# Fourth chunk's mask ahead of waiting sums, warm matmuls, and output matmuls of the second token tile over the end of the first

## The chip, the cores and the metric

One core of a Trainium2 chip. The time is device microseconds (us) of one execution; the profile's span is about 1.8 us shorter (230.7 against 232.52 for the profiled execution of the kernel before). PE is TensorE, PEld its weight loads, DVE VectorE, ACT ScalarE, POOL GpSimd.

## The reference, cut to what matters

```python
for t in range(S):                                   # decayed linear attention, 8 heads, S = 768, D = 64
    state = gamma * state + outer(k[t], v[t])
    y[t] = scale * q[t] @ state
x = y as (3072 tokens, 512)
h = x @ w_in                                         # 512 -> 2048
g = h + sin(alpha * h) ** 2 / (alpha + 1e-9)
out = g @ w_out                                      # 2048 -> 512
```

## The kernel before

The attention is done in 24 chunks of 128 tokens. `stage_T` (or two `half_T`) transposes q and k of a chunk, `stage_A` makes the scores `pa` and masks them on DVE into `aT`, `stage_M` multiplies with v into `py` and copies the result to `xT`. Chunks are gathered in groups (4, 2, 4, ... chunks); for each group the feed-forward layer runs over 16 blocks f of 128 hidden units:

```python
def ff_in(g, f, square, cols=None):
    ph = psum.tile([128, hi - lo], F32, name="ph", tag="mm", bufs=4)     # ring of four PSUM banks
    s = work.tile([128, hi - lo], F32, name="s", tag="s", bufs=4)
    for i in range(KS):
        nc.tensor.matmul(ph, w_in[:, i, ...f...], xT[g][:, i, lo:hi], ...)
    nc.scalar.activation(out=s, in_=ph, func=ACTF.Sin, scale=alpha_sb[:, f:f + 1])
    if square == "A":  nc.scalar.activation(out=s, in_=s, func=ACTF.Square)
    else:              nc.vector.tensor_mul(s, s, s)
    return lambda: nc.vector.scalar_tensor_tensor(gT[g][:, f, lo:hi], s, rec_alpha, ph, ...)   # "the sum"

def ff_out(g, ts, f):                       # one output matmul po; po also takes a bank of the ring "mm"
    nc.tensor.matmul(po[g, ts], gT[g][:, f, ts * C:(ts + 1) * C], w_out[:, f, :], ...)
```

"The sum of f" below is that last DVE instruction, which also frees the bank of ph. The first group has no earlier group to hide behind. Its first three chunks run through f = 0 to 5 while the fourth chunk (`e3`) arrives; then the fourth chunk's 128 columns run through f = 0 to 5 (`second tile`), then all 512 columns through f = 6 to 15:

```python
decay_table(3)
for f in range(4):
    ff_in(0, f, "AAD"[f % 3], (0, n3))()
half_T(e3, 0, nc.vector); half_T(e3, 1, nc.vector)
idle_work(2)                                # 2 matmuls on zeros, the "warm matmuls"
for f in range(4, early):
    ff_in(0, f, "AAD"[f % 3], (0, n3))()    # the trailing () issues the sum at once
    if f == 4:
        stage_A(e3)
stage_M(e3); decay_table(4); idle_work(3)
for f in range(early):
    ff_in(0, f, "AD"[f % 2], (n3, 4 * C))()
    if f in (2, 3, 4, 5):
        ff_out(0, 0, f - 2)
# ... scaling of v, two memsets, decay_table(5)
phase(0, [... ff_out(0, 0, f) for f in range(4, FF - 2)], {}, "AAD", range(early, FF))
outs = [... ff_out(0, 0, f) for f in range(FF - 2, FF)] + out_pieces(0, (1, 2, 3))
fill(9); stage_T(P[4]); scale_v(P[4], nc.vector); fill(5); stage_A(P[4])   # fill(n): n items of outs
```

Of the kernel before, what the change touches and what calls it, by code (L numbers as in the profile page):

```python
# [15 lines left out]
def kernel(  # L16
# [15 lines left out]
    nc = tc.nc  # L32
    B, H, S, D = q.shape
    C = 128
# [6 lines left out]
    FF = d_ff // 128  # L41
# [64 lines left out]
    def scale_v(j, eng):  # L106
        eng.tensor_mul(raw["v", j], raw["v", j], kg[:, j % NCH, :, None].to_broadcast([128, H, D]))  # L107
# [51 lines left out]
    def decay_table(c):  # L159
        nc.vector.tensor_mul(qg[:, c], qg[:, 0], step[:, c, :, None].to_broadcast([128, NP, C]))  # L160
# [11 lines left out]
    def half_T(j, i, eng):  # L172

        if i == 0:
            st["qkT", j] = work.tile([128, 2 * NP, 128], BF16, name="qkT", tag="qkT", bufs=3)
        pt = psum.tile([128, NP, 128], BF16, name="pt", tag="mm", bufs=4)
        for p in range(NP):
            nc.tensor.transpose(pt[:, p, :], raw["qk"[i], j][:, 2 * p:2 * p + 2, :].rearrange("p h d -> p (h d)"), ident)
        o = st["qkT", j][:, i * NP:(i + 1) * NP, :]
        if eng is nc.scalar:  # L180
            nc.scalar.copy(o, pt)
        else:
            nc.vector.tensor_copy(o, pt)

    def stage_T(j):
        pt = psum.tile([128, 2 * NP, 128], BF16, name="pt", tag="ty")
        st["qkT", j] = work.tile([128, 2 * NP, 128], BF16, name="qkT", tag="qkT", bufs=3)
        for i in range(2):
            for p in range(NP):
                nc.tensor.transpose(pt[:, i * NP + p, :],  # L190
                                    raw["qk"[i], j][:, 2 * p:2 * p + 2, :].rearrange("p h d -> p (h d)"), ident)
        nc.vector.tensor_copy(st["qkT", j], pt)  # L192

    def stage_A(j):
        qkT = st["qkT", j]
        pa = psum.tile([128, 2, NP, 128], F32, name="pa", tag="pa")
        for p in range(NP):
            for e in range(2):
                r = slice(64 * e, 64 * e + 64)
                nc.tensor.matmul(pa[:, e, p, :], qkT[r, NP + p, :], qkT[r, p, :],  # L200
                                 start=(p == 0), stop=True, skip_group_check=True)
        aT = work.tile([128, 2, NP, 128], BF16, name="aT", tag="aT", bufs=2)
        m = dec.rearrange("p e n t -> p (e n) t") if j % NCH == 0 else mask_bc
        nc.vector.tensor_mul(aT.rearrange("p e n t -> p (e n) t"), pa.rearrange("p e n t -> p (e n) t"), m)  # L204
        st["aT", j] = aT

    def stage_S(j):
        c = j % NCH
        if c == 0:
            st["ps"] = psum.tile([128, NP, D], F32, name="ps", tag="ps")  # L210
        ps = st["ps"]
        for p in range(NP):
            for e in range(2):
                nc.tensor.matmul(ps[64 * e:64 * e + 64, p, :], raw["k", j][:, 2 * p + e, :], raw["v", j][:, 2 * p + e, :],  # L214
                                 start=(c == 0 and p == 0), stop=True, skip_group_check=True)
        return ps

    def keep_S(j, ps):
        for e in range(2):
            r = slice(64 * e, 64 * e + 64)  # L220
            nc.scalar.copy(s_bd[(j % NCH + 1) % 2][r, :, r], ps[r, :, :])  # L221

    def stage_M(j):
        c = j % NCH
        g, i = place[j]
        if g not in xT:
            xT[g] = work.tile([128, KS, sizes[g] * C], BF16, name="xT", tag="xT", bufs=3)
        qkT, aT, vs = st["qkT", j], st["aT", j], raw["v", j]
        py = psum.tile([128, NP, 128], F32, name="py", tag="ty")
        if c > 0:  # L230
            for p in range(NP):
                for e in range(2):
                    r = slice(64 * e, 64 * e + 64)
                    nc.tensor.matmul(py[r, p, :], s_bd[c % 2][:, p, r], qkT[:, p, :],  # L234
                                     start=(p == 0), stop=True, skip_group_check=True)
        for p in range(NP):
            for e in range(2):
                nc.tensor.matmul(py[64 * e:64 * e + 64, p, :], vs[:, 2 * p + e, :], aT[:, e, p, :],  # L238
                                 start=(c == 0 and p == 0), stop=True, skip_group_check=True)
        x = xT[g][:, :, i * C:(i + 1) * C]  # L240
        if c == 0:
            nc.scalar.copy(x, py)
            return
        ps = stage_S(j) if c < NCH - 1 else None
        nc.vector.tensor_mul(x, py, qg[:, c])  # L245
        if ps is not None:
            keep_S(j, ps)
# [4 lines left out]
    def ff_in(g, f, square, cols=None):  # L252
        n = sizes[g] * C
        lo, hi = cols or (0, n)
        if g not in gT:
            gT[g] = work.tile([128, FF, n], BF16, name="gT", tag="gT", bufs=2)
        ph = psum.tile([128, hi - lo], F32, name="ph", tag="mm", bufs=4)
        s = work.tile([128, hi - lo], F32, name="s", tag="s", bufs=4)
        for i in range(KS):
            nc.tensor.matmul(ph, w_in[:, i, f * 128:(f + 1) * 128], xT[g][:, i, lo:hi],  # L260
                             start=(i == 0), stop=(i == KS - 1))
        nc.scalar.activation(out=s, in_=ph, func=ACTF.Sin, scale=alpha_sb[:, f:f + 1])  # L262
        if square == "A":
            nc.scalar.activation(out=s, in_=s, func=ACTF.Square)  # L264
        else:
            nc.vector.tensor_mul(s, s, s)
        return lambda: nc.vector.scalar_tensor_tensor(  # L267
            gT[g][:, f, lo:hi], s, rec_alpha[:, f:f + 1], ph, op0=ALU.mult, op1=ALU.add)
# [5 lines left out]
    def ff_out(g, ts, f):  # L274
        if f == 0:
            po[g, ts] = psum.tile([128, d_model], F32, name="po", tag="mm", bufs=4)
        nc.tensor.matmul(po[g, ts], gT[g][:, f, ts * C:(ts + 1) * C], w_out[:, f, :],  # L277
                         start=(f == 0), stop=(f == FF - 1))
        if f == FF - 1:
            o_sb = work.tile([128, d_model], F32, name="o_sb", tag="o_sb", bufs=3)  # L280
            o_dram = out_view[:, groups[g][ts], :]
            if (g, ts) == end:
                h = d_model // 2
                nc.vector.tensor_copy(o_sb[:, :h], po[g, ts][:, :h])
                nc.scalar.copy(o_sb[:, h:], po[g, ts][:, h:])
            else:
                nc.scalar.copy(o_sb, po[g, ts])  # L287
            nc.sync.dma_start(out=o_dram, in_=o_sb)

    def out_pieces(g, tss):  # L290
        return [lambda ts=ts, f=f: ff_out(g, ts, f) for ts in tss for f in range(FF)]
# [5 lines left out]
    def idle_work(n):  # L297
        for _ in range(n):
            nc.tensor.matmul(spare["ps"], warm[:, :128], warm, start=True, stop=True)  # L299
# [5 lines left out]
    e0, e1, e2, e3 = order[:B]  # L305
# [41 lines left out]
    def phase(g, outs, att, squares, slots=range(FF)):  # L347

        no, n0, done = len(outs), len(slots), 0
        for n, f in enumerate(slots):  # L350
            add = ff_in(g, f, squares[f % len(squares)])
            for fn in att.get(f, ()):
                fn()
            add()
            while done < no * (n + 1) // n0:
                outs[done]()
                done += 1
# [18 lines left out]


    n3, early = 3 * C, 6
    decay_table(3)
    for f in range(4):  # L380
        ff_in(0, f, "AAD"[f % 3], (0, n3))()
    half_T(e3, 0, nc.vector)
    half_T(e3, 1, nc.vector)
    idle_work(2)
    for f in range(4, early):
        ff_in(0, f, "AAD"[f % 3], (0, n3))()
        if f == 4:
            stage_A(e3)
    stage_M(e3)
    decay_table(4)  # L390
    idle_work(3)
    for f in range(early):
        ff_in(0, f, "AD"[f % 2], (n3, 4 * C))()
        if f in (2, 3, 4, 5):
            ff_out(0, 0, f - 2)
    scale_v(e0, nc.vector)
    for t in s_bd:
        nc.vector.memset(t, 0.0)
    decay_table(5)
    P = order  # L400
    phase(0, [lambda f=f: ff_out(0, 0, f) for f in range(4, FF - 2)], {}, "AAD", range(early, FF))
    outs = [lambda f=f: ff_out(0, 0, f) for f in range(FF - 2, FF)] + out_pieces(0, (1, 2, 3))

    def fill(n):
        for _ in range(n):
            outs.pop(0)()
# [7 lines left out]
        if n in (13, 15, 17):  # L414
            scale_v(order[(n - 11) // 2], nc.gpsimd)

    fill(9)
    stage_T(P[4])
    scale_v(P[4], nc.vector)
    fill(5)  # L420
# [7 lines left out]
    stage_M(P[4])  # L428
    fill(6)
    stage_M(P[5])  # L430
    fill(4)
    phase(1, outs,
          {0: [T(P[6])], 2: [A(P[6])], 3: [T(P[7])], 5: [A(P[7]), M(P[6])], 7: [T(P[8])],
           9: [A(P[8]), M(P[7])], 11: [T(P[9])], 13: [A(P[9]), M(P[8]), SK(P[9] - 1)], 15: [M(P[9])]}, "A")
# [46 lines left out]
```

## Time and profile before

| | before |
|---|---|
| median of four runs | 231.68 us (231.13 to 232.51) |
| span of the profile | 230.7 us |
| PE busy | 94% |
| PE waits before 46 us that could move | 1.92, 0.99 and 0.63 us |
| half clock | one stretch of 3.41 us, 25.75 to 29.16 us |

A line of the timeline reads: start in us, length in us, engine, line of the program, instruction, output<-inputs, shapes, number of instructions merged; in brackets the idle time of the engine before it and what ended it. The prediction shows the lines for the waits and the clock. What it shows only in numbers is the loop f = 6 to 15; here it is for f = 9 in the timeline of the kernel before:

```profile
33.00 1.03 PE L260 MATMUL ph<-xT,w_in 128*128 128x512 bf16 x4
34.07 0.69 ACT L262 ACTIVATE s<-ph,alpha_sb 128x512 f32<-128x512 f32 x1 [0.52 <-PE ph L260]
34.79 0.63 ACT L264 ACTIVATE s<-s 128x512 f32<-128x512 f32 x1
35.45 0.75 DVE L267 SCALAR_TENSOR_TENSOR gT<-s,rec_alpha,ph 128x512 bf16<-128x512 f32 x1 [0.31 <-ACT s L264]
36.29 0.38 PE L277 MATMUL po<-w_out,gT 128*128 128x512 bf16 x1
36.51 1.03 PE L260 MATMUL ph<-xT,w_in 128*128 128x512 bf16 x4
```

ph of f = 9 starts at 33.00; its sine, square and sum follow one after another; po of f = 9 can start only when the sum has ended (36.20), and ph of f = 12 stands behind it. From ph to ph of three f later: 3.51 us, 1.17 per f, though PE's own work is 1.08.

### The profile page before, as it was taken

Reading aid. Unit: us, or ns where it says so; the run is one execution under the profiler, and the core shown is the slowest. Engines: PE = TensorE matmul, PEld = TensorE weight load, DVE = VectorE, ACT = ScalarE, POOL = GpSimd, SP = SyncE. Lnnn points to the kernel's source line nnn. Section 1 sums busy time; section 2 is a strip of 40 time slices with the busy share of each in tenths; the row PEclk is TensorE's granted clock in tenths of the full one; section 3 lists DMA queues with packets and bytes.
Section 4 is the critical chain, followed back from the end, with each engine's and each line's share of the span. In section 5 each row is a group of like instructions: output and inputs, shape, how many; then the busy total and the mean of one; then the engine's idle time right before and its main releaser. Section 6 shows DMA issues by size and latency. Waiting matters only on the chain.

```text
span 230.7 us, 4496 instructions
## 1 busy us (share of the span) xinstructions
PE 217.7 (94%) x1786; PEld 115.0 (50%) x1786; DVE 143.6 (62%) x234; ACT 167.2 (72%) x323; POOL 90.3 (39%) x105
## 2 busy tenths in 40 slices
PE   7995799799999999999999999999999999999992
PEld 3542543356775555545454544554544454556540
DVE  4776887595987777866575755674764554533400
ACT  7786479436898899877787777787677878777720
POOL 8955437899999999992000000000000000000000
PEclk9999799999999999999999999999999999999999
DMA  9999999999999999996110110011011011111111
GB/s 130 150 190 198 205 199 156 154 186 135 139 94 126 115 91 154 107 124 57 45 48 8 40 47 24 24 47 45 3 45 48 0 45 45 48 45 45 50 66 70
DMA packets 82613, 20.49 MB, mean 89 GB/s; under 512 B 75408, under 2 KB 79520, under 8 KB 82592
## 3 DMA queue, kind: packets, MB, share of 16 engines
q0 software_dynamic: 77024, 13.37, 74.2%
q1 hardware_dynamic: 5568, 6.83, 8.7%
q8 instruction: 14, 0.23, 0.4%
q14 instruction: 7, 0.06, 0.1%
HBM read 27.27 MB, written 6.29 MB: 145 GB/s over the span
## 4 chain that ended last, share of the span: by engine, by line
PE 79%; DVE 7%; DMA 4%; POOL 4%; ACT 4%; issue 1%; POOLq 0%
PE po L277 36%; PE ph L260 31%; DMA kr<-in_k_dram 4%; PE pt L190 4%; PE pa L200 2%; PE py L234 2%; DVE aT L204 2%; DVE gT L267 2%; ACT s L262 2%; PE py L238 2%; ACT s L264 1%; POOL vr L78 1%; POOL qr L78 1%; DVE xT L245 1%; PE ps L214 1%
## 5 line engine op out<-in xcount | busy, mean ns | idle before, releaser
L267 DVE SCALAR_TENSOR_TENSOR gT<-s,rec_alpha,ph 128x512 bf16<-128x512 f32 (+3 forms) x118 | 75.8, 646 | 63.2 <-ACT s L264 62.4
L277 PE MATMUL po<-w_out,gT 128*128 128x512 bf16 x384 | 103.1, 382 | 2.1 <-DVE gT L267 1.9
L260 PE MATMUL ph<-xT,w_in 128*128 128x512 bf16 (+3 forms) x472 | 102.6, 343 | 0.4 <-DVE xT L245 0.3
L262 ACT ACTIVATE s<-ph,alpha_sb 128x512 f32<-128x512 f32 (+3 forms) x118 | 71.2, 605 | 37.0 <-PE ph L260 35.9
L260 PEld LDWEIGHTS <-w_in 128*128 128x128 bf16 x472 | 46.3, 100 | 44.5 <-issue 2.3
L264 ACT ACTIVATE s<-s 128x512 f32<-128x512 f32 (+3 forms) x110 | 61.0, 555 | 3.5
L277 PEld LDWEIGHTS <-gT 128*128 128x128 bf16 x384 | 35.3, 98 | 36.7 <-DVE gT L267 5.5
L204 DVE TENSOR_TENSOR aT<-pa,mask 128x1024 bf16<-128x1024 f32 x20 | 24.4, 1222 | 0.9 <-PE pa L200 0.8
L107 POOL TENSOR_TENSOR vr<-vr,kg 128x512 bf16<-128x512 bf16 x21 | 22.7, 1095 | 2.8 <-DMA vr<-in_v_dram 2.8
L78 POOL DMA_DIRECT2D qr<-in_q_dram x23 | 21.3, 926 | 4.8 <-DMA w_in<-in_moe_w_in_dram 1.7
L78 POOL DMA_DIRECT2D vr<-in_v_dram x24 | 21.8, 909 | 3.0 <-DMA w_in<-in_moe_w_in_dram 1.7
L78 POOL DMA_DIRECT2D kr<-in_k_dram x23 | 20.6, 894 | 3.5 <-DMA w_out<-in_moe_w_out_dram 3.4
L221 ACT CAST s_bd<-ps 64x256 bf16<-64x256 f32 x40 | 14.4, 360 | 7.1 <-PE ps L214 6.8
L192 DVE COPY qkT<-pt 128x1024 bf16<-128x1024 bf16 x20 | 13.8, 689 | 5.4 <-PE pt L190 4.9
L287 ACT COPY o_sb<-po 128x512 f32<-128x512 f32 x23 | 13.3, 580 | 4.5 <-PE po L277 4.5
L245 DVE TENSOR_TENSOR xT<-py,qg 128x512 bf16<-128x512 f32 x20 | 13.7, 684 | 2.3 <-PE py L238 2.2
L299 PE MATMUL spare<-warm 128*128 128x512 bf16 x33 | 10.9, 449 | 1.2 <-DVE warm L126 1.2
L238 PE MATMUL py<-aT,vr 128*64 128x128 bf16 x192 | 9.5, 219 | 2.3 <-DVE aT L204 2.3
L200 PEld LDWEIGHTS <-qkT 64*128 64x128 bf16 x192 | 5.4, 94 | 9.2 <-issue 5.7
L200 PE MATMUL pa<-qkT 64*128 64x128 bf16 x192 | 9.5, 219 | 0.4 <-DVE dec L311 0.2
L234 PE MATMUL py<-qkT,s_bd 128*64 128x128 bf16 x160 | 8.3, 225 | 0.4 <-DVE xT L245 0.4
L238 PEld LDWEIGHTS <-vr 128*64 128x64 bf16 x192 | 6.9, 110 | 3.2 <-issue 2.9
(62 smaller groups left out, 95.2 us busy)
## 6 DMA issues: line engine op xcount, KB each, us to landing
out_dram<-o_sb SPq DMA_DIRECT2D x24, 256.0 KB, 2.0
vr<-in_v_dram POOLq DMA_DIRECT2D x24, 128.0 KB, 4.9
qr<-in_q_dram POOLq DMA_DIRECT2D x23, 128.0 KB, 4.4
kr<-in_k_dram POOLq DMA_DIRECT2D x23, 128.0 KB, 4.8
w_in<-in_moe_w_in_dram POOLq DMA_DIRECT2D x4, 512.0 KB, 10.7
w_out<-in_moe_w_out_dram POOLq DMA_DIRECT2D x4, 512.0 KB, 14.9
q<-in_q_dram SPq DMA_DIRECT2D x1, 256.0 KB, 3.4
k<-in_k_dram SPq DMA_DIRECT2D x1, 256.0 KB, 4.1
```

The source lines that it names most:

```text
L78: nc.gpsimd.dma_start(out=t, in_=chunk_of(src, j))
L107: eng.tensor_mul(raw["v", j], raw["v", j], kg[:, j % NCH, :, None].to_broadcast([128, H, D]))
L200: nc.tensor.matmul(pa[:, e, p, :], qkT[r, NP + p, :], qkT[r, p, :], start=(p == 0), stop=True, skip_group_check=True)
L204: nc.vector.tensor_mul(aT.rearrange("p e n t -> p (e n) t"), pa.rearrange("p e n t -> p (e n) t"), m)
L221: nc.scalar.copy(s_bd[(j % NCH + 1) % 2][r, :, r], ps[r, :, :])
L238: nc.tensor.matmul(py[64 * e:64 * e + 64, p, :], vs[:, 2 * p + e, :], aT[:, e, p, :], start=(c == 0 and p == 0), stop=True, skip_group_che ...
L245: nc.vector.tensor_mul(x, py, qg[:, c])
L260: nc.tensor.matmul(ph, w_in[:, i, f * 128:(f + 1) * 128], xT[g][:, i, lo:hi], start=(i == 0), stop=(i == KS - 1))
L262: nc.scalar.activation(out=s, in_=ph, func=ACTF.Sin, scale=alpha_sb[:, f:f + 1])
L264: nc.scalar.activation(out=s, in_=s, func=ACTF.Square)
L267: return lambda: nc.vector.scalar_tensor_tensor(gT[g][:, f, lo:hi], s, rec_alpha[:, f:f + 1], ph, op0=ALU.mult, op1=ALU.add)
L277: nc.tensor.matmul(po[g, ts], gT[g][:, f, ts * C:(ts + 1) * C], w_out[:, f, :], start=(f == 0), stop=(f == FF - 1))
```

## The change

Its intent: take the fourth chunk's mask out from behind sums that wait for ACT, keep PE's clock up meanwhile, and put matmuls that are ready over the end of the first tile, where po14 and po15 wait for the last sums. The core of the diff:

```diff
-    decay_table(3)
-    for f in range(4):
-        ff_in(0, f, "AAD"[f % 3], (0, n3))()
-    half_T(e3, 0, nc.vector)
-    half_T(e3, 1, nc.vector)
-    idle_work(2)
-    for f in range(4, early):
-        ff_in(0, f, "AAD"[f % 3], (0, n3))()
+    adds = []
+    for f in range(early):
+        adds.append(ff_in(0, f, "AADAAA"[f], (0, n3)))
+        if f == 0:
+            decay_table(3)
+        if f in (1, 2):
+            adds.pop(0)()
+        if f == 3:
+            idle_work(2)
+            stage_T(e3)
+            idle_work(1)
+            adds.pop(0)()
         if f == 4:
             stage_A(e3)
+            adds.pop(0)()
+    idle_work(2)
+    adds.pop(0)()
     stage_M(e3)
-    decay_table(4)
+    adds.pop(0)()
     idle_work(3)
     for f in range(early):
-        ff_in(0, f, "AD"[f % 2], (n3, 4 * C))()
-        if f in (2, 3, 4, 5):
+        add = ff_in(0, f, "AD"[f % 2], (n3, 4 * C))
+        if f > 1:
             ff_out(0, 0, f - 2)
+        add()
+    decay_table(4)
 ... (scaling, memsets, decay_table(5): unchanged)
-    phase(0, [... range(4, FF - 2)], {}, "AAD", range(early, FF))
-    outs = [... ff_out(0, 0, f) for f in range(FF - 2, FF)] + out_pieces(0, (1, 2, 3))
+    phase(0, [... range(4, FF - 2)], {}, "AD", range(early, FF))
+    outs = out_pieces(0, (1, 2, 3))
+    outs[9:9] = [... ff_out(0, 0, f) for f in range(FF - 2, FF)]
-    fill(9)
+    fill(7)
 ... (stage_T(P[4]) to fill(6): unchanged)
     stage_M(P[5])
-    fill(4)
+    fill(3)
```

## The prediction

> **What bounds it.** I read, in this order, the page (busy times, clock row), the timeline of TensorE (PE) with its waits, the timeline of all engines from 14 to 46 us, the windows view, and the instruction order of both programs. First two lines of the page, then the waits in PE's timeline (start, length, what, idle before and its releaser; us):
>
> ```profile
> PE 217.7 (94%) x1786; PEld 115.0 (50%) x1786; DVE 143.6 (62%) x234; ACT 167.2 (72%) x323; POOL 90.3 (39%) x105
> PEclk9999799999999999999999999999999999999999
> ...
> 18.09 0.40 PE L178 MATMUL pt<-ident,qr 128*128 128x128 bf16 x4 [0.45 <-DMA qr<-in_q_dram]
> 19.83 0.40 PE L178 MATMUL pt<-ident,kr 128*128 128x128 bf16 x4 [1.34 <-DMA kr<-in_k_dram]
> 24.32 0.41 PE L238 MATMUL py<-aT,vr 128*64 128x128 bf16 x8 [1.92 <-DVE aT L204]
> 32.77 0.39 PE L277 MATMUL po<-w_out,gT 128*128 128x512 bf16 x1 [0.27 <-DVE gT L267]
> 42.42 0.39 PE L277 MATMUL po<-w_out,gT 128*128 128x512 bf16 x1 [0.99 <-DVE gT L267]
> 43.44 1.90 PE L277 MATMUL po<-w_out,gT 128*128 128x512 bf16 x8 [0.63 <-DVE gT L267]
> ```
>
> PE is the bound, and from 46 us on it hardly waits: the same list has only four more waits, 0.18, 0.17, 0.34 and 0.24 us, at 66, 71, 72 and 97 us. All that a reordering can win lies before 46 us, plus those four. The change touches nothing before 17 us, and the k chunk of the fourth sequence ("kr") is issued by POOL, so it lands at 19.8 us in both kernels. The movable waits are 1.92 us for the masked scores, and 0.99 + 0.63 us at the end of the first group. How the 1.92 us arises, in the timeline of all engines (L267 is the sum that makes gT of one f, L260 its ph, L277 the output matmul po):
>
> ```profile
> 20.15 0.75 DVE L183 COPY qkT<-pt 128x512 bf16<-128x512 bf16 x2
> 20.50 0.81 PE L260 MATMUL ph<-xT,w_in 128*128 128x384 bf16 x4
> 21.24 0.40 PE L200 MATMUL pa<-qkT 64*128 64x128 bf16 x8
> 21.96 0.52 ACT L264 ACTIVATE s<-s 128x384 f32<-128x384 f32 x1
> 22.52 0.61 DVE L267 SCALAR_TENSOR_TENSOR gT<-s,rec_alpha,ph 128x384 bf16<-128x384 f32 x1 [1.61 <-ACT s L264]
> 23.05 1.22 DVE L204 TENSOR_TENSOR aT<-pa,dec 128x1024 bf16<-128x1024 f32 x1
> ```
>
> The scores pa are finished at 21.6 us, but the mask starts at 23.05, because the sum of f=4 stands ahead of it on VectorE (DVE) and waits for a sine and a square. The clock follows, seen in the windows view cut every 3.41 us:
>
> ```profile
> 18.93:22.34 3.41, 2.51 (x22) 1.28 (x23) 1.94 (x5) 1.47 (x3) 1.90 (x3) 1.00 1.27 205
> 22.34:25.75 3.41, 1.49 (x19) 0.99 (x19) 3.20 (x5) 1.26 (x3) 1.22 (x2) 1.00 1.24 207
> 25.75:29.16 3.41, 3.41 (x25) 2.40 (x23) 2.04 (x7) 2.54 (x8) 1.41 (x2) 0.50 1.24 206
> ```
>
> First number after the length is PE busy, the one before the last two is the clock: with PE busy 1.49 of 3.41 us, the next 3.41 us run at half clock, where the four 128x128 matmuls of one f and its output matmul take 0.43 us each instead of 0.22.
>
> **What the skill says.** "TensorE: Matmul & The Clock Gate", The HAM clock gate: half clock by default, full after a busy window, windows of 3413 ns that run free of the kernel. The trace agrees: one stretch of 0.50, 3.4 us long, after the emptiest window. As the phase is free, I expect that not every execution of the kernel before has this stretch. Same page, Architectural detail: ScalarE (ACT) and VectorE take their instructions strictly in order. The trace agrees (the mask above). "PSUM — Partial Sum Buffer", Specifications: eight banks. Four of them are the ring "mm"; while one holds the output sum po, three are left to ph.
>
> **Part 1, fourth chunk.** After: ph0 to ph3, two warm matmuls (filling the wait for qr), the eight transposes behind the k landing (to 20.23), one warm, ph4, pa, ph5, two warm, py, three warm. On DVE: one copy of 1024 columns (later such rows: 0.69 us) instead of two (0.75), 20.28 to 20.97; the sum of f=2 (0.57) to 21.5. pa can start at 21.02 and is read complete at 21.47. The mask (1.22) then runs 21.5 to 22.72 instead of 23.05 to 24.28; py starts at 22.77 (was 24.32) and ends at 23.18. ACT has sine and square of f=5 until 23.35, since f=5 is now squared there, so the copy of xT (0.58) runs 23.3 to 23.88, and the second token tile's first ph starts at **23.93 instead of 25.41: 1.48 us earlier**. PE idles only some 0.2 us here besides the k wait, so the clock should stay full.
>
> **Part 2, second tile (f=0 to 5, 128 columns).** At full clock ACT and the wait for a free bank set the pace. With sine 0.37, square 0.31, DVE square 0.28, sum 0.35 and 0.05 from one engine to another, I get the sums ending at 25.45, 26.03, 26.3, 27.0, 27.59 and 28.17: 4.24 us from first ph to last sum, against 25.41 to 30.37 = 4.96 at half clock: **0.72 us won**. The table of chunk 4 (L160), which ran in DVE's shadow at 25.30, now stands behind the last sum with the scaling, two memsets and the other table. By the starts in the trace (30.02 sum, 30.29, 30.98, 31.44, 31.98) that queue was 1.96 us and becomes 2.50: **0.54 lost**. The sum of f=6 starts at 27.82 + 2.50 = 30.32 instead of 31.98, 1.66 earlier. The weights are there: POOL's waits put the landings of the second w_out piece at 27.95 and of the last w_in at 30.5, and I need them at 27.95 and 34.9.
>
> **Part 3, f=6 to 15.** Per f, PE needs 0.86 + 0.22 = 1.08; DVE with one square in two 1.02; ACT 0.91 (before 1.02). None is the pace. It is the loop through a bank: sum 0.75, 0.05, po 0.22, ph of f+3 1.03, 0.04, sine to square 0.72, square to sum 0.66: 3.47 us for three f (3.53 if DVE squares), 1.17 per f. Before: (42.63 - 31.98)/9 = 1.18, which this explains. So "AD" in place of "AAD" wins nothing here; it adds squares to DVE's queue. Stepping f by f with these numbers I get the sum of f=15 from 41.40 to 42.15, against 42.63 to 43.38: **1.23 us earlier** (0.43 of the 1.66 is lost again).
>
> **Part 4, the end covered.** PE issues po13 at 39.5, then seven matmuls of the second tile to 41.26, the transposes of chunk P4 to 41.71, two more, and po14 and po15 at 42.14 and 42.36, when both sums exist. No wait of 0.99 or 0.63 is left. The next limit is DVE: sum f=15 to 42.15, copy of P4's transposes (0.69) to 42.79, pa of P4 at 42.84. PE arrives there at 42.79, so the two meet. Before, pa of P4 started at 46.80, with 14 output matmuls done since po13 where the new one has 12: 46.80 - 42.84 - 2 x 0.217 = **3.5 us won at this point**.
>
> **Part 5, group 1.** One more output matmul is left over, three in all, and 19 instead of 16 are spread over its slots; same PE work, 0.65 us of it moved. Doubles fall behind slots 5, 10 and 15, ahead of the waits of 0.18 and 0.34: I count 0.3 won, and 0.06 lost where 3 instead of 4 matmuls cover the last xT. After that everything shifts rigidly.
>
> Sum on the profiled span: 3.5 + 0.3 - 0.06 = 3.7 us, so 230.7 becomes some 227.0. But the profiled execution took 232.52, and the three timed ones 231.69, 231.66 and 232.51. I take the 0.83 us between the two values as the half-clock stretch, which the median escapes; then Part 2's 0.72 is not won against the median. Both ways: 231.69 - (3.7 - 0.72) = 228.7; 227.0 + (232.52 - 230.7) = 228.8. I go a little below for what my loop may overstate: **228.6 us, 1.3% faster**.
>
> **Rivals.** First, the wait only moves: PE is ready earlier, but the bank loop and DVE's longer queue hand it back before 43 us. For: 0.43 us of it is in my own steps, and DVE squares five of ten instead of three. Against: the covering removes 1.6 us of waiting whatever the loop does. It would leave some 1.5 to 2 us, 229.7 to 230.2. Second, more is won: AD unloads ACT, phase 3 gets down to PE's 1.08 per f, 0.9 us more, and the warm clock is worth its full 0.7 against the median too: 227.0 to 227.7, near 2%. Against: the loop has no slack at 1.17. Third, DMA takes over: chunks arrive at POOL's pace whatever PE does, and POOL is busy to 104 us. Against: the tightest need I find, the state of chunk e1 at 69.10, follows its scaling by about 5 us, more than the shift. Fourth, a half-clock stretch appears elsewhere, as after the wait for k (1.34 us idle): one costs some 0.8 us, and would give 229.4.
>
> **Range and chances.** The first and fourth rival set the upper end, the second the lower: 227.3 to 229.9. Faster by over 2% needs 227.06 or less, for which two of my terms must be too small together: 0.08. Slower by over 2% has no mechanism: 0.01. Within 2%: 0.91.
>
> **What would show it.** py of the fourth chunk near 22.8 us; no clock under 0.9 after it; the first 128-column ph near 23.9; the sum of f=6 near 30.3 and of f=15 near 41.4; no PE wait over 0.3 us between 39 and 47; pa of P4 near 42.8; the waits at 66 and 72 us (then 62 and 68) smaller. Wrong would be: the mask still behind a sum; a new wait for DVE's copy or for a bank after f=15; the gain gone between 43 us and the end; or timed runs that still come in two values 0.8 apart.

## The result, and the profile after

The kernel after takes **228.42 us** (median of four runs, 228.21 to 228.58), against 231.68. The ratio is 0.9856 with a 95% interval of 0.9825 to 0.9887. Ratios here are the mean time of one kernel's fast runs over that of the other's fast runs of the same rounds, so they are not quite the ratio of the medians. The output is correct.

Two lines of the page after, then lines of PE's timeline:

```profile
PE 212.8 (94%) x1759; PEld 113.9 (50%) x1789; DVE 143.4 (63%) x234; ACT 166.5 (74%) x322; POOL 89.9 (40%) x105
PEclk9999999999999999999999999999999999999999
...
18.70 0.40 PE L190 MATMUL pt<-ident,qr 128*128 128x128 bf16 x4 [0.22 <-DMA qr<-in_q_dram]
19.51 0.40 PE L190 MATMUL pt<-ident,kr 128*128 128x128 bf16 x4 [0.41 <-DMA kr<-in_k_dram]
22.43 0.41 PE L238 MATMUL py<-aT,vr 128*64 128x128 bf16 x8
23.56 0.83 PE L260 MATMUL ph<-xT,w_in 128*128 128x128 bf16 x12
25.12 0.38 PE L260 MATMUL ph<-xT,w_in 128*128 128x128 bf16 x4 [0.52 <-DVE gT L267]
27.99 0.38 PE L277 MATMUL po<-w_out,gT 128*128 128x512 bf16 x1 [0.29 <-DMA w_out<-in_moe_w_out_dram]
30.81 0.39 PE L277 MATMUL po<-w_out,gT 128*128 128x512 bf16 x1 [0.50 <-DVE gT L267]
39.22 1.89 PE L277 MATMUL po<-w_out,gT 128*128 128x512 bf16 x8
42.58 0.40 PE L200 MATMUL pa<-qkT 64*128 64x128 bf16 x8
```

The wait of 1.92 us ahead of py and the waits of 0.99 and 0.63 us at the end of the tile are gone; py starts at 22.43 instead of 24.32, and the output matmuls from 39.22 run without a wait. Three waits are new or larger: 0.52 us in the second tile for the sum that frees a bank of the ring (Part 2 of the prediction counts with such a wait), 0.29 us for the second piece of w_out, and 0.50 us for the sum of f = 6. This trace lacks some 30 PE records (1759 matmuls where 1789 weights were loaded), so idle times of 0.16 us put down to "issue" in it are most likely gaps of the record; the profile of squares_back, with 1789 of both, has none of them.

Why py is earlier, in the timeline of all engines after:

```profile
20.71 0.40 PE L200 MATMUL pa<-qkT 64*128 64x128 bf16 x8
21.15 1.23 DVE L204 TENSOR_TENSOR aT<-pa,dec 128x1024 bf16<-128x1024 f32 x1
22.29 1.66 DVE L267 SCALAR_TENSOR_TENSOR gT<-s,rec_alpha,ph 128x384 bf16<-128x384 f32 x3
```

The mask starts 0.44 us after the start of pa, where it was 1.81 us before (21.24 to 23.05), and the three sums that wait for ACT come behind it. And the windows of the kernel after, cut at its own clock phase, counted back from its clock change at 226.03 us (length, then busy us of PE, PEld, DVE, ACT and POOL with counts, then clock, DMA share and GB/s):

```profile
17.90:21.30 3.40, 2.71 (x25) 1.37 (x25) 2.52 (x6) 2.41 (x5) 2.69 (x4) 1.00 1.53 199
21.30:24.70 3.40, 3.17 (x30) 1.74 (x29) 2.65 (x4) 2.83 (x8) 1.43 (x2) 1.00 1.24 206
24.70:28.10 3.40, 2.49 (x19) 1.44 (x20) 3.00 (x10) 2.48 (x8) 0.87 (x1) 1.00 1.24 206
```

No window is as empty as the one of 1.49 us before, and the clock stays at 1.00.

How far the stations moved, read from the starts in both timelines:

| start of | before | after | earlier by |
|---|---|---|---|
| k transposes of the fourth chunk (DMA) | 19.83 | 19.51 | 0.32 |
| mask of the fourth chunk | 23.05 | 21.15 | 1.90 |
| first 128-column ph | 25.41 | 23.56 | 1.85 |
| sum of f=6 | 31.98 | 30.02 | 1.96 |
| sum of f=15 | 42.63 | 41.11 | 1.52 |
| pa of chunk P4 | 46.80 | 42.58 | 4.22 (2 output matmuls fewer done: 3.79) |
| first ph of group 1 | 54.07 | 49.70 | 4.37 (3 fewer: 3.72) |
| first ph of group 2 | 72.39 | 68.07 | 4.32 |
| end | 230.75 | 226.43 | 4.32 |

### The profile page after: what moved, and what is told of

The parts are those of the page before. It is cut to its first block, busy times and chain, and to the rows that moved or that the text cites. A ratio compares the mean times of both kernels' runs of the same rounds, so it can differ in the third digit from the quotient of the medians.

```text
span 226.4 us, 4471 instructions
## 1 busy us (share of the span) xinstructions
PE 212.8 (94%) x1759; PEld 113.9 (50%) x1789; DVE 143.4 (63%) x234; ACT 166.5 (74%) x322; POOL 89.9 (40%) x105
## 4 chain that ended last, share of the span: by engine, by line
PE 79%; DVE 8%; ACT 4%; DMA 3%; POOL 3%; issue 2%; POOLq 0%; ACTq 0%
PE po L277 34%; PE ph L260 32%; PE pt L190 4%; DMA w_in<-in_moe_w_in_dram 3%; DVE gT L267 3%; PE pa L200 3%; PE py L234 3%; PE py L238 2%; ACT s L262 2%; DVE aT L204 2%; ACT s L264 1%; POOL vr L78 1%; PE ps L214 1%; DVE s L266 1%; DVE xT L245 1%
## 5 line engine op out<-in xcount | busy, mean ns | idle before, releaser
L260 PE MATMUL ph<-xT,w_in 128*128 128x512 bf16 (+3 forms) x470 | 101.4, 339 | 2.3 <-DVE gT L267 1.1
L277 PE MATMUL po<-w_out,gT 128*128 128x512 bf16 x358 | 96.3, 379 | 3.3 <-issue 1.9
L260 PEld LDWEIGHTS <-w_in 128*128 128x128 bf16 x472 | 45.3, 98 | 46.0 <-issue 3.1
L264 ACT ACTIVATE s<-s 128x512 f32<-128x512 f32 (+3 forms) x109 | 60.3, 553 | 3.5
L192 DVE COPY qkT<-pt 128x1024 bf16<-128x1024 bf16 x21 | 14.5, 689 | 3.3 <-PE pt L190 3.0
L190 PEld LDWEIGHTS <-qr 128*128 128x128 bf16 x84 | 6.4, 98 | 4.7 <-DMA qr<-in_q_dram 0.7
```

The costliest lines, as they stand in the source:

```text
L190: nc.tensor.transpose(pt[:, i * NP + p, :], raw["qk"[i], j][:, 2 * p:2 * p + 2, :].rearrange("p h d -> p (h d)"), ident)
L260: nc.tensor.matmul(ph, w_in[:, i, f * 128:(f + 1) * 128], xT[g][:, i, lo:hi], start=(i == 0), stop=(i == KS - 1))
```

## The experiments

Twelve kernels ran, in three batches of four, each batch on one chip with the kernel before beside them (33 runs of it in all). The DMA landing of the fourth chunk's k moves between executions: its transposes started between 18.42 and 20.82 us in the profiles below, and everything behind moves with it. So stations of different profiles are compared from the start of the mask, unless said otherwise.

### Part 1 alone (front_only)

The new loop for f = 0 to 5, with the rest of the kernel before:

```diff
-    decay_table(3)
-    for f in range(4): ...            (the old loop, as in the diff above)
+    adds = [] ...                     (the new loop, down to stage_M(e3) and the last adds.pop(0)())
     decay_table(4)
     idle_work(3)
```

> The kernel before with Part 1 alone (sums delayed, transposes in one bank, mask ahead of waiting sums, five warm matmuls, f=5 squared on ScalarE); second tile, squares and end as before. My steps: first 128-column ph near 23.6 instead of 25.4, full clock, and the waits of about 0.99 and 0.63 us at the end still there. Against executions of the kernel before without a half-clock stretch 1.3 to 1.6 us faster (about 230.2); against one with it 2.2. The rival (the bank loop and VectorE hand the gain back) expects under 0.7 us.

Median 230.22, mean 230.16 us, ratio 0.9911 (0.9871 to 0.9951); no run had a clock under 0.997. Of the eleven runs of the kernel before beside it, seven had a clock of 0.996 or more and a mean of 231.68; against those Part 1 is worth 1.51 us. In its PE timeline the two waits at the end stand as before:

```profile
40.46 0.39 PE L277 MATMUL po<-w_out,gT 128*128 128x512 bf16 x1 [0.99 <-DVE gT L267]
41.38 1.90 PE L277 MATMUL po<-w_out,gT 128*128 128x512 bf16 x8 [0.53 <-DVE gT L267]
```

The gain is kept to the end, so the rival "handed back before 43 us" falls for this part.

### The covered end alone (end_only)

```diff
-    outs = [... range(FF - 2, FF)] + out_pieces(0, (1, 2, 3))
+    outs = out_pieces(0, (1, 2, 3))
+    outs[9:9] = [... range(FF - 2, FF)]
-    fill(9)
+    fill(7)
...
-    fill(4)
+    fill(3)
```

> The kernel before with the end covering alone (nine matmuls of the second token tile ahead of po14 and po15, fills of 7 and 3). My steps: the waits of 0.99 and 0.63 us go, pa of chunk P4 starts near 44.4, 2.0 us won there, 0.3 more in group 1: about 2.3 us faster, 229.4. The rival (VectorE's copy of the next chunk, which stands behind the last sum, takes the wait over) expects under 1 us.

Median 229.00, mean 229.26 us, ratio 0.9874 (0.9837 to 0.9911): 2.4 us against the same seven runs (2.6 without its one run at a clock of 0.993). pa of P4 started at 44.67 us. So the covering is the larger part of the gain. Its profiled execution, the longest at 230.28 us, fell to half clock again, after a window with little PE work, and at another phase than the kernel before:

```profile
20.91:24.32 3.41, 1.57 (x15) 0.67 (x14) 2.53 (x6) 1.68 (x3) 1.75 (x3) 1.00 1.24 208
24.32:27.74 3.42, 3.41 (x24) 2.26 (x24) 1.81 (x4) 1.47 (x5) 0.91 (x2) 0.50 1.24 206
```

### Warm matmuls alone (warm_only)

```diff
+    idle_work(6)
     stage_M(e3)
     decay_table(4)
```

> The kernel before with six warm matmuls (1.3 us, inside the 1.92 us wait) ahead of py of the fourth chunk. If the two values of the timed runs (231.7 and 232.5) come from the half-clock stretch: no clock under 0.9 in the profile, no run over 232, median 231.0 to 231.7. If they come from something else (DMA landings): still runs near 232.5, and a median within 0.2 us of the kernel before.

Median 231.62, mean 231.70 us, ratio 0.9979 (0.9943 to 1.0016); no clock under 0.997 in six runs, but one run at 232.46 with a clock of 1.0. The mean equals that of the kernel before at full clock (231.68). In the kernel before, 8 of 33 runs had a clock of 0.992 or less; their mean is 233.15 us, that of the other 25 is 231.67. Six runs without a low clock are few, since seven of eleven of the kernel before in the same rounds had none either; the profile says more. The window that was 1.49 us busy is 3.25 us busy here (22.01 to 25.43), no half clock follows it, and from the start of the mask to the end it is 206.96 us where the kernel before has 207.70. So the stretch is real, filling PE's wait removed it, and it cost 0.74 us to the end. But it is not the only spread: full-clock runs reach 232.87 as well, and low-clock runs are longer by 1.48 us, twice the stretch. A late landing of k would lengthen a run and also leave PE idle; no timed run shows its landing, so this stays open. The expected "no run over 232" was a miss.

### Squares as before (squares_back)

```diff
-    phase(0, [...], {}, "AD", range(early, FF))
+    phase(0, [...], {}, "AAD", range(early, FF))
```

> The kernel after with the squares of f=6 to 15 as before (AAD instead of AD). My Part 3 says that a loop of ph, sine, square, sum and po sets the pace, not ScalarE: 228.4 give or take 0.3. The rival (ScalarE's load was the pace) expects 0.6 to 1 us slower, 229.0 to 229.4.

Median 228.08 us, ratio 0.9826 (0.9791 to 0.9862), against 0.9857 for the kernel after in other rounds: not slower, and within the intervals not surely faster. In the profiles the sums of f = 6 to 15 come every 1.18 us (29.41 to 40.05) where the kernel after has 1.23 (30.02 to 41.11): 0.45 us over the nine steps. ACT's load was not the pace, and the extra squares on DVE cost rather than gain. At pa of P4 only 0.16 of the 0.45 us is left (21.27 us from the mask, against 21.43), because the covering matmuls had hidden most of it.

### The loop: bank, order, and both (after_again, bank, lag, bank_lag)

The kernel after ran again beside three variants:

> The kernel after, unchanged, as the measure for the three beside it: 228.4, ratio 0.984 to 0.988.

Median 228.35, mean 228.47 us, ratio 0.9857 (0.9822 to 0.9892). The bank variant:

```diff
-        ph = psum.tile([128, hi - lo], F32, name="ph", tag="mm", bufs=4)
+        if g == 0 and cols is None and f in (9, 13):
+            ph = psum.tile([128, hi - lo], F32, name="ph", tag="ps")
+        else:
+            ph = psum.tile([128, hi - lo], F32, name="ph", tag="mm", bufs=4)
```

> The kernel after; ph of f=9 and f=13 take the bank of tag ps, so that four banks serve ph in f=6 to 15. My Part 3 names the loop ph, sine, square, sum, po, ph of f+3; po(n) stands ahead of ph(n+3) in TensorE's order, so the sum of n gates ph(n+3) with or without a free bank: no change against the kernel after, within 0.3 us. If the bank alone is what holds ph back, 0.5 to 0.9 us faster.

Mean 228.70 us, ratio 0.9860 (0.9827 to 0.9893); sums every 1.23 us as in the kernel after. The order variant:

```diff
-    phase(0, [... range(4, FF - 2)], {}, "AD", range(early, FF))
+    phase(0, [... range(4, FF - 3)], {}, "AD", range(early, FF))
-    outs[9:9] = [... range(FF - 2, FF)]
+    outs[9:9] = [... range(FF - 3, FF)]
...
-    fill(3)
+    fill(4)
```

> The kernel after; po stands one f later in TensorE's order (po(n) after ph(n+3), po13 moved to the covering matmuls, last fill 4). With three banks ph(n+3) still needs the bank that the sum of n frees: no change within 0.3 us if the bank holds the loop as well; 0.5 to 0.9 us faster if the order of po alone did.

Its five timed runs have a mean of 228.16 us, ratio 0.9844 (0.9811 to 0.9876): 0.3 us under the kernel after beside it, within the noise. Its profiled run was slow (see the end) and gives no stations. Both together:

> Both together. If Part 3's loop is the pace, its two links (bank and order) fall only together: the pace from the sum of f=6 to that of f=15 goes from 1.23 us per f toward TensorE's 1.08, 0.5 to 1.3 us faster than the kernel after, 227.1 to 227.9. If VectorE's queue or ACT is the pace, no change.

Median 227.47, mean 227.60 us, ratio 0.9820 (0.9788 to 0.9851): 0.87 us under the kernel after of the same rounds. The sums of f = 6 to 15 come every 1.06 us (30.15 to 39.70). The bank alone left them at 1.23, and neither link alone changed the time beyond noise; the pace with the order alone was not seen, as its profile was slow. The intervals of the times overlap, but the profiles decide: from the mask to the end both together take 204.43 us, where the kernel after takes 205.28 and repeats it within 0.02 us (after_again, bank, no_warm). That is what a loop through both links predicts.

But the gain was larger on the way than at the end. From the mask, pa of P4 came 1.61 us earlier than in the kernel after (19.82 against 21.43; with one output matmul, 0.22 us, more still to do, 1.39), while the first ph of group 2 came only 0.84 earlier (46.08 against 46.92). PE's timeline of this variant shows two waits in which the difference can have gone, and POOL's what it waited for:

```profile
64.13 0.32 PE L214 MATMUL ps<-vr,kr 128*64 128x64 bf16 x8 [0.52 <-POOL vr L107]
67.36 0.81 PE L263 MATMUL ph<-xT,w_in 128*128 128x512 bf16 x3 [0.27 <-DVE xT L245]
...
63.00 2.07 POOL L107 TENSOR_TENSOR vr<-vr,kg 128x512 bf16<-128x512 bf16 x2
```

The state of chunk e1 needs v scaled by POOL, which runs at its own pace; PE is now early enough to wait for it. In the kernel after, POOL does this at 63.26 us and PE shows no such wait.

### Without the warm matmuls (no_warm)

```diff
         if f == 3:
-            idle_work(2)
             stage_T(e3)
-            idle_work(1)
             adds.pop(0)()
...
-    idle_work(2)
     adds.pop(0)()
     stage_M(e3)
```

> The kernel after without its five warm matmuls between ph3 and py of the fourth chunk (two, one, two). If the earlier mask alone keeps TensorE busy enough: no half-clock stretch after 22 us, 228.4 within 0.3. If the warm matmuls are what keeps the clock: a stretch of 0.5 in some executions and those about 0.7 us longer.

Median 228.11 us, ratio 0.9857 (0.9807 to 0.9906). Five of six runs had a clock of 0.998 or more and a mean of 228.18 us; one had 0.989 and took 230.77. The ten runs of the kernel after had none under 0.996. So the warm matmuls cost nothing that shows. That they also protect the clock is likely but not shown: one such run in six is few.

### The two tables later (tables_later)

```diff
-    decay_table(4)
     scale_v(e0, nc.vector)
...
-    decay_table(5)
...
     stage_M(P[4])
+    decay_table(4)
     fill(6)
     stage_M(P[5])
+    decay_table(5)
```

> The kernel after with the decay tables of chunks 4 and 5 (0.69 and 0.63 us of VectorE) moved from ahead of the sum of f=6 to behind the two stage_M of chunks P4 and P5, where VectorE idles. By Part 2's term the sum of f=6 starts near 29.1 instead of 30.0; with the loop behind it 0.3 to 0.6 us faster than the kernel after. If VectorE's queue there has slack: no change.

Mean 228.54 us, ratio 0.9849 (0.9814 to 0.9883): no gain. The sum of f = 6 did start at 29.02 us, but the sums then came every 1.28 us, so at pa of P4 0.20 us was left (21.23 from the mask), and a wait of about that size stands further on:

```profile
48.34 0.41 PE L234 MATMUL py<-qkT,s_bd 128*64 128x128 bf16 x8 [0.28 <-DVE xT L245]
```

DVE's queue ahead of f = 6 is real, as long as the prediction said, and worth nothing while the loop behind it sets the pace.

### All three, with either mix of squares (all_three, all_three_aad)

Edit: the diffs of bank, lag and tables_later together; all_three_aad has "AAD" in `phase(0, ...)` as well.

> Bank, lag and later tables together: the sum of f=6 near 29.1 and 1.08 to 1.12 us per f from there: 1 to 2 us faster than the kernel after, 226.5 to 227.5. If the landing of the weights (second w_out piece near 28.0) holds po4, the gain stops at about 1.

> The same with AAD squares. Once the loop is gone the engines' own loads count: ACT 1.02 per f and VectorE 0.95 against 0.91 and 1.02 with AD, TensorE 1.08: within 0.3 us of all_three either way.

Means 227.75 and 227.57 us, ratios 0.9815 (0.9778 to 0.9851) and 0.9807 (0.9773 to 0.9841). They and bank_lag cannot be told apart by their times (from the mask to the end the profiles take 204.18, 204.16 and 204.43 us). All three are faster than both kernels, by 0.7 to 0.9 us in the means against after_again, which for two of them ran in other rounds. The 1 to 2 us expected of all_three were a miss; in its profile PE waits 0.22 us for w_out at 33.66 us. The sum of f = 15 comes 1.8 and 2.1 us earlier from the mask than in the kernel after (18.15 and 17.87 against 19.96), and the wait for POOL's scaling takes part of it back (0.45 us in all_three).

## Why the prediction was right

The predicted 228.6 us and the measured 228.42 are 0.2 apart; the change is within 2% as forecast, and the mechanism of each part was found in the traces.

- **Part 1.** Expected: mask from 21.5, first 128-column ph at 23.93. Measured 21.15 and 23.56 with k landing 0.32 us earlier than assumed, so the length from k to ph was 4.05 against 4.10. That k lands at 19.8 us in both kernels was a premise that did not hold; the landing moves. Alone Part 1 gave 1.51 us.
- **Part 2.** First ph to the end of the last sum: expected 4.24 us, measured 23.56 to 27.80, 4.24. DVE's queue behind it: expected 2.50, measured 27.45 to 30.02, 2.57.
- **Part 3.** Expected 11.08 us from the sum of f = 6 to that of f = 15; measured 11.09 (before 10.65). "AD wins nothing" held; bank_lag showed that the loop is the pace.
- **Part 4.** pa of P4 expected at 42.84, measured 42.58; won there 3.5 expected, 3.79 measured, of which 0.32 is the earlier landing. The covering alone gave 2.4 us. Part 1 alone and the covering alone add up to 3.9, more than the 3.2 us of both in the kernel after (231.68 against 228.47). Little of that is AD's: squares_back, of the same rounds as the two parts alone and without AD, gained 3.5 us, and its profile is 0.15 us shorter from the mask to the end (205.13 against 205.28). What makes up the rest is not shown; timed runs of one kernel spread by over 1 us, so it can be noise.
- **Part 5.** 0.3 expected; measured between the first ph of group 1 and of group 2: 18.32 us before and 18.37 after, with three matmuls (0.65 us) more, so 0.60 won. This term was too small by half: it counted 0.3 for the waits of 0.18 and 0.34 us, and in the kernel after both are gone from PE's timeline.
- **The step from profile to median.** The prediction took the spread of 0.83 us between timed runs for the half-clock stretch, which the median escapes. The stretch had the size that it gave, 0.72: 0.74 us by the profiles of the kernel before and of warm_only. But "two values" was wrong. Full-clock runs of the kernel before lie anywhere from 230.98 to 232.87, and the low-clock ones are longer by 1.48 us on average, not by 0.72 or 0.83; the other cause of spread stays open (see warm_only). More than one stretch per run is not needed to explain the clocks: a stretch of 3.41 us lowers the mean clock over 231 us by 0.007, and a half clock at the very end, where PE has no work left, by up to 0.004 more (from 223.50 us on in all_three_aad). One of each can make up 0.988 to 0.992; only the run at 0.981 needs more.
- **The sum.** The profile after ends 4.32 us earlier. Less 0.32 for the landing of k and 0.74 for the stretch, 3.26 us are left, which is the difference of the medians too (that it agrees to the last digit is luck). The prediction's counterpart is 3.7 - 0.72 = 3.0; Part 5 was too small by the missing 0.3. Going "a little below" made up for 0.1 of it, and its reason, a loop that might be overstated, was not the true one: the loop measured 11.09 against 11.08.
- **Rivals.** "Handed back" was right for the 0.43 us of Part 3 alone. "More is won through AD" was wrong. "DMA takes over" showed as 0.29 us ahead of po4, where the landing expected at 27.95 let po4 start at 27.99; what it cost was not measured. The half-clock stretch elsewhere did not come: none of the ten runs of the kernel after has a clock under 0.996. "POOL's scaling becomes the wait" came true only in the faster variants.

## What to carry to other kernels

When a chain of engines feeds back into the engine that bounds the kernel, write the loop out link by link and compare its length with each engine's load; removing one of two parallel links (a bank, or the place in the queue) did nothing that could be measured here until the other was removed too. A wait at the end of a stage is best covered with matmuls whose inputs are long ready, and that paid more here than speeding the stage up. Put an instruction that others wait for ahead of those that themselves wait in an in-order queue, and look which later producer (here POOL's scaling) the earlier consumer will meet next.

## What the Trainium skill lacked or had wrong

- "TensorE: Matmul & The Clock Gate" (The HAM clock gate; Why this matters for your kernels) gives the window's length and warns of idle gaps of more than some 3 us, but does not say how empty a window must be. Here windows with PE busy 1.49 and 1.57 of 3.41 us (44 and 46%) were followed by half clock, though the longest gap in the first was 1.92 us; one with 1.89 (55%; bank, 18.90 to 22.31) was not, nor those of 2.49 us and more in the kernel after.
- The same page (Seeing it yourself) says that the trace events of the clock gate are unreliable and that the gate has been seen stuck for over 50 us. One profile (lag) goes further: it holds no clock event, its clock reads 1.000, and yet PE ran at about half speed for the whole 440.7 us, though busy 97% of it:

```profile
PE 427.7 (97%) x1759; PEld 174.1 (40%) x1789; DVE 145.9 (33%) x234; ACT 172.4 (39%) x322; POOL 90.3 (20%) x105
L277 PE MATMUL po<-w_out,gT 128*128 128x512 bf16 x360 | 191.2, 676 | 4.5 <-issue 4.5
```

  The mean of one output matmul is 676 ns there and 379 ns in the kernel after; back to back they start 443 ns apart there and 216 ns in the kernel after. What set it off stays open; the five timed runs of the same kernel were normal.
- No page read tells how much the landing of a transfer moves between executions of one program: the same k chunk could be transposed from 18.42 us in one profile and from 20.82 in another, which is as large as the larger effects here.
